# Fp16 halves of an attention kernel: a buffer and a DMA transpose per tile instead of per pair of tiles

## The chip, the cores and the metric

The kernel runs on 1 core of one Trainium2 chip. The metric is the time of one execution on the device in microseconds (us), the median of several runs; lower is better. A core has TensorE (PE, its weight loads PEld), VectorE (DVE), ScalarE (ACT), GpSimd (POOL) and SyncE (SP), which here only issues DMAs. Each engine works off its own instructions in order, and semaphores tie them together.

## The reference

Bucketed attention, then a mixing layer with a two-dimensional Fourier transform and a feed-forward network, then a gated layer:

```python
# q, k, v: (2, 8, 768, 64); proj: (64, 6); d_model = 512
q_bucket = np.sum((q @ proj > 0) * powers, axis=-1)      # the same for k
mask = q_bucket[:, :, :, None] == k_bucket[:, :, None, :]
scores = np.where(mask, scale * q @ k.T, -1e9)
attn = softmax(scores)
x = (attn @ v), heads side by side                       # (2, 768, 512)

mixed = np.real(fft(fft(x, axis=1), axis=2))
u = x + mixed
un = layer_norm(u)
x = u + np.maximum(un @ w_ch1, 0.0) @ w_ch2              # 512 -> 2048 -> 512

gate = sigmoid(causal depthwise convolution of x, 5 taps)
out = (gate * (x @ w_val)) @ w_out
```

## The kernel before

Matrix products are made in fp16 with each operand split into two halves, a high one (the value rounded to fp16) and a low one (the rest). Attention runs once for each of the two batches, `attention(b, ...)`. Of a batch's 8 heads two are taken together: a group `g` of 4. In a group the 768 query rows are three units `i` of two tiles of 128 rows; for each unit and each head `hh` of the group `pair` (L316) makes the softmax weights of two tiles `j`, and `unit_out` (L356) multiplies both heads' weights by the values `vt`.

One tile in `pair`: 4 matmuls into `sc` (L324), DVE moves the scores to `e` and takes the row maximum (L336), ACT makes the exponentials in `e` (L341) and then the high half in `a` (L345, by `copy_of`, L112), and POOL subtracts it from `e` to give the low half, in two instructions of 384 columns (L348, by `both`, L120). When both tiles of the pair are there, one DMA transpose issued by SP brings the whole of `a` (128 rows, 24 blocks of 128 columns) into `at` (L353). At 4 of the 48 places (`TPE`) the transpose is made by TensorE instead, in `by_pe` (L222): 24 transposes into three PSUM tiles of 1024 columns, and three copies by ACT. `unit_out` then runs 36 matmuls into `pv` (L362), which need all of `at` of both heads.

`prep(g)` (L230) does the like for a group's queries and keys: ACT writes the high halves of q and k into `st`, DVE (in part POOL) the low halves (L126, L120), one DMA transpose brings both into `tb` (L247), DVE copies parts of it to `ta` (L116), and matmuls into `bt` (L259) give the bucket codes. One group (`PPE`) goes by `by_pe`; the first group has its own `prep_first` (L279).

The pool `a` holds the buffers of `a` and `st`: 3 that last through both batches and 1 more during the first batch (L890, L894). `e` has 4 buffers in the first batch and 2 in the second; `at` 4 and 2.

SP issues every DMA of this part: the loads of q, k, v, the blocks of the large weights (`ring`, L431), which DVE, ACT and POOL turn into fp16 halves (L417 to L419 and the helpers), and the transposes. A `ring` load waits until its slot has been read. While the second batch's attention runs, TensorE works on the first batch's feed-forward matmuls (L710, L727). The program is built with a scheduler that orders each engine's instructions by an estimate of its own; `issue_after` fixes a few orders by hand.

## Time and profile before

| what | value |
|---|---|
| median of 3 runs | 696.27 us (696.04 to 697.73) |
| span of the profiled execution | 692.9 us |
| PE busy | 571.7 us, 83% |
| DVE busy | 518.3 us, 75% |
| ACT busy | 368.2 us, 53% |
| POOL busy | 290.5 us, 42% |
| DMA transposes `at<-a` | 44, median 5.9 us from issue to landing |
| DMA transposes `tb<-st` | 6, median 6.0 us |

The span runs from the first to the last instruction in one profiled execution; the time of a run is 3.4 us longer than that span. Busy shares are averages over stages of different kinds: to about 172 us the first batch's attention, then its mixing layer beside weights and the start of the second batch, to about 412 us the second batch's attention beside feed-forward matmuls, and then matrix products nearly alone.

### The profile page before, as it was taken

To read this page: it belongs to the slowest core of one execution; us is meant where nothing else is said; L and a number is where in the kernel's file an instruction comes from. 1 tells how busy PE (TensorE), PEld (TensorE's weight loads), DVE (VectorE), ACT (ScalarE), POOL (GpSimd) and SP (SyncE) were. 2 spreads that over 40 slices of the span, in tenths; PEclk is the share of its full clock that TensorE was granted. 3 is DMA by queue.
4 is the path that set the end of the run, shared out by engine and by line. 5 is a ranking of instruction groups with operands and counts; after the bars stand their busy time and mean duration, and the time that the engine had idled before them with its cause. 6 is when DMAs were issued, how large, how long until landed. Compare 5 with 4: busy or idle time off the path is not lost.

```text
span 692.9 us, 13096 instructions
## 1 busy us (share of the span) xinstructions
PE 571.7 (83%) x5078; PEld 439.0 (63%) x5078; DVE 518.3 (75%) x1007; ACT 368.2 (53%) x747; POOL 290.5 (42%) x312
## 2 busy tenths in 40 slices
PE   6667748677634868988789999899899999999997
PEld 2343516465423646766568789789676788888864
DVE  6888678778999888999965529987899346282582
ACT  4997779986765435876588815321244202111242
POOL 2857568875668523876556510244232100000000
PEclk9696859877866889999999999999999999999999
DMA  8879799895787452779667774100000000000001
GB/s 297 207 138 238 154 228 216 168 198 127 130 171 153 115 149 89 145 147 195 126 128 138 138 166 152 65 1 2 2 31 30 32 1 1 1 2 1 1 31 61
DMA packets 176284, 75.79 MB, mean 109 GB/s; under 512 B 160864, under 2 KB 166624, under 8 KB 176224
## 3 DMA queue, kind: packets, MB, share of 16 engines
q1 hardware_dynamic: 175648, 74.88, 48.6%
q8 instruction: 39, 0.64, 0.4%
q14 instruction: 21, 0.17, 0.1%
q10 hardware_dynamic: 576, 0.10, 0.1%
HBM read 32.50 MB, written 3.15 MB: 51 GB/s over the span
## 4 chain that ended last, share of the span: by engine, by line
PE 33%; DVE 30%; DMA 14%; issue 10%; POOL 7%; ACT 5%; SPq 0%; ACTq 0%; POOLq 0%; DVEq 0%
PE f L727 13%; DMA at<-a 8%; PE f L710 8%; POOL a L120 6%; DVE e L336 3%; DVE wt L417 3%; DVE wt L418 3%; PE pv L362 3%; DMA ring<-in_moe_w_ch_dram 3%; DVE gt L752 3%; DMA tb<-st 2%; PE op L871 2%; DVE wt L419 2%; ACT e L341 2%; PE vp L846 1%
## 5 line engine op out<-in xcount | busy, mean ns | idle before, releaser
L120 POOL TENSOR_TENSOR a<-e,a 128x384 f16<-128x384 f32 x184 | 177.0, 985 | 94.2 <-ACT a L112 60.9
L710 PE MATMUL f<-un,w 128*128 128x256 f16 x1152 | 137.5, 276 | 2.8 <-DVE h L692 2.4
L727 PE MATMUL f<-h,w 128*128 128x256 f16 x1152 | 131.6, 273 | 2.5 <-ACT w L112 2.5
L710 PEld LDWEIGHTS <-w 128*128 128x128 f16 x1152 | 113.7, 99 | 23.1 <-issue 5.1
L727 PEld LDWEIGHTS <-w 128*128 128x128 f16 x1152 | 111.8, 98 | 19.6 <-ACT w L112 2.8
L336 DVE TENSOR_SCALAR_CACHE_REDUCE e<-sc 128x768 f32<-128x768 f32 x96 | 91.0, 951 | 21.9 <-POOL a L120 17.4
L362 PE MATMUL pv<-at,vt 128*64 128x256 f16 x864 | 69.1, 304 | 39.8 <-DMA at<-a 32.3
L341 ACT ACTIVATE e<-e,mx 128x768 f32<-128x768 f32 x96 | 89.3, 931 | 3.8
L362 PEld LDWEIGHTS <-vt 128*64 128x64 f16 x864 | 56.2, 122 | 47.3 <-issue 31.3
L112 ACT ACTIVATE a<-e 128x768 f16<-128x768 f32 x96 | 80.3, 839 | 1.6 <-DMA at<-a 0.9
L324 PE MATMUL sc<-ta 96*128 96x384 f16 x192 | 54.8, 369 | 27.8 <-DVE e L336 24.7
L692 DVE SCALAR_TENSOR_TENSOR h<-f,h 128x512 f16<-128x512 f32 x48 | 32.7, 687 | 32.1 <-ACT h L691 32.0
L324 PE MATMUL sc<-tb 128*128 128x384 f16 x192 | 54.9, 370 | 0.0
L691 ACT ACTIVATE h<-f 128x512 f16<-128x512 f32 x48 | 28.3, 589 | 46.1 <-PE f L710 46.0
L120 POOL TENSOR_TENSOR w<-wt,w 128x256 f16<-128x256 f32 x40 | 31.3, 788 | 39.3 <-ACT w L112 39.3
L324 PEld LDWEIGHTS <-ta 96*128 96x128 f16 x192 | 17.4, 103 | 47.0 <-issue 40.6
L112 ACT ACTIVATE x<-xb 128x256 f16<-128x256 f32 x24 | 11.7, 536 | 62.5 <-DVE xb L698 61.1
L698 DVE SCALAR_TENSOR_TENSOR xb<-f,xb 128x256 f32<-128x256 f32 x24 | 13.7, 619 | 38.7 <-PE f L727 38.6
L340 ACT ACTIVATE mx<-mx 128x1 f32<-128x1 f32 x96 | 18.5, 197 | 39.4 <-DVE e L336 38.8
L417 DVE TENSOR_SCALAR wt<-ring 128x256 int32<-128x256 int32 (+1 forms) x60 | 32.5, 546 | 8.6 <-DMA ring<-in_moe_w_ch_dram 8.5
L418 DVE SCALAR_TENSOR_TENSOR wt<-ring,wt 128x256 int32<-128x256 int32 (+1 forms) x60 | 38.0, 638 | 0.6
L819 DVE SCALAR_TENSOR_TENSOR gt<-xb,cw,gt 128x256 f32<-128x256 f32 x60 | 37.3, 683 | 0.0
(147 smaller groups left out, 918.6 us busy)
## 6 DMA issues: line engine op xcount, KB each, us to landing
ring<-in_moe_w_ch_dram SPq DMA_DIRECT2D x40, 256.0 KB, 3.1
ring<-in_moe_w_ch_dram SPq DMA_DIRECT2D x12, 512.0 KB, 5.5
lv<-in_v_dram SPq DMA_DIRECT2D x8, 384.0 KB, 3.9
out_dram<-ob SPq DMA_DIRECT2D x12, 256.0 KB, 2.0
lq<-in_q_dram SPq DMA_DIRECT2D x7, 384.0 KB, 3.8
lk<-in_k_dram SPq DMA_DIRECT2D x7, 384.0 KB, 4.0
ring<-in_moe_w_val_dram SPq DMA_DIRECT2D x4, 512.0 KB, 4.1
ring<-in_moe_w_out_dram SPq DMA_DIRECT2D x4, 512.0 KB, 3.6
```

What stands on the lines that cost most here:

```text
L112: return nc.scalar.activation(out=o, in_=i, func=ACTF.Copy, scale=s)
L120: return (nc.gpsimd if eng == "g" else nc.vector).tensor_tensor(out=o, in0=i0, in1=i1, op=op)
L324: nc.tensor.matmul(out=s[:, n, 0:384], lhsT=z[0:rows, 0, hh, r], rhs=z[0:rows, 1, hh, n * 384:n * 384 + 384], start=(x == 0), stop=(x == 1),)
L336: nc.vector.tensor_scalar(e.rearrange("p (a b) -> p a b", a=2), s, -(PEN * PEN) / 2, None, ALU.max, ALU.max, accum_out=m[:, 0:1]).ins
L341: marks["first", 2 + j] = nc.scalar.activation(out=e, in_=e, func=ACTF.Exp, bias=m[:, 1:2], scale=SC, accum_out=sums[:, hh, j:j + 1]).ins
L362: nc.tensor.matmul(out=p[64 * hh:64 * hh + 64, :], lhsT=va[g][:, hh, c, x, :], rhs=at[hh][:, :, y, c, :], start=(c == 0 and n == 0), stop= ...
L417: nc.vector.tensor_scalar(tmp, hi, 3, 0x3FFFFFF8, ALU.logical_shift_left, ALU.bitwise_and)
L418: nc.vector.scalar_tensor_tensor(out=tmp, in0=hi, scalar=-0x40000000, in1=tmp, op0=ALU.bitwise_and, op1=ALU.bitwise_or)
L692: nc.vector.scalar_tensor_tensor(out=h[:, 1, f:f + 2, :], in0=p, scalar=0.0, in1=h[:, 0, f:f + 2, :], op0=ALU.max, op1=ALU.subtract)
L710: nc.tensor.matmul(out=p[:, o, :], lhsT=w1[:, i, kd, (f + o) * 128:(f + o) * 128 + 128], rhs=un[:, j, kd, :], start=(k == 0), stop=(k == 3 ...
L727: nc.tensor.matmul(out=p[:, o, :], lhsT=w2[:, i, f, (d + o) * 128:(d + o) * 128 + 128], rhs=h[:, j, f, :], start=(k == 0), stop=(k == 3 * ...
L819: nc.vector.scalar_tensor_tensor(out=o, in0=src, scalar=cw[:, d, j:j + 1].bitcast(FP32), in1=o, op0=ALU.mult, op1=ALU.add)
```

## The change

`a` becomes a buffer of one tile (both halves, 12 blocks of 128 columns), with 6 lasting buffers and 2 more in the first batch, so that the memory is the same. Each tile has a DMA transpose of its own into its half of `at`, issued for tile 0 without waiting for tile 1. `st` becomes two such buffers, one for q and one for k, each with its own transpose into its half of `tb`. `by_pe` handles one tile: two PSUM tiles of 768 columns and two copies, so four copies for a pair instead of three. The number of DMA transposes goes from 50 to 100; their bytes stay.

```diff
-TPE = {(0, g, i, 1): 'aaa' for g in range(4) for i in (1,)}
-PPE = {(0, 1): 'aaa'}
+TPE = {(0, g, i, 1): 'a' for g in range(4) for i in (1,)}
+PPE = {(0, 1): 'a'}
...
-        def by_pe(ot, it, how):
-            for o in range(0, 4 * S, 1024):
-                p = P.bt.tile([128, 1024], FP16, tag="g", name="atp") if b else P.tp.tile([128, 1024], FP16, tag="tp", name="atp")
-                for c in range(0, 1024, 128):
+        def by_pe(ot, it, eng):
+            for o in range(0, 2 * S, S):
+                p = P.tp.tile([128, 1024], FP16, tag="tp", name="atp")
+                for c in range(0, S, 128):
                     nc.tensor.transpose(p[:, c:c + 128], it[:, o + c:o + c + 128], P.idh)
-                i = copy_of(ot[:, o:o + 1024], p, 1.0, how[o // 1024])
+                i = copy_of(ot[:, o:o + S], p[:, 0:S], 1.0, eng)
             return i.ins
...
-                st = P.a.tile([128, 2, 2 * C, 2, D], FP16, tag="a", name="st", lasting=b and g == 0)
-                copy_of(st[:, 0, :, 1, :], lq, QS, "a")
-                copy_of(st[:, 1, :, 0, :], lk, QS, "a")
-                rest_of(st[:, 0, :, 0, :], st[:, 0, :, 1, :], lq, QS, REST[b][0])
-                rest_of(st[:, 1, :, 1, :], st[:, 1, :, 0, :], lk, QS, REST[b][1])
+                st = [P.a.tile([128, 2 * C, 2, D], FP16, tag="a", name="st", lasting=b and g == 0) for _ in range(2)]
+                for y, x in enumerate((lq, lk)):
+                    copy_of(st[y][:, :, 1 - y, :], x, QS, "a")
+                for y, x in enumerate((lq, lk)):
+                    rest_of(st[y][:, :, y, :], st[y][:, :, 1 - y, :], x, QS, REST[b][y])
...
-            if (b, g) in PPE:
-                it, ot = st.rearrange("p a c x d -> p (a c x d)"), tb.rearrange("p a h t -> p (a h t)")
-                marks[b, "prep", g] = by_pe(ot, it, PPE[b, g])
-            else:
-                marks[b, "prep", g] = nc.sync.dma_start_transpose(
-                    out=tb.rearrange("p a h (c t) -> p (a h c) t", t=128), in_=st.rearrange("p a c x d -> p (a c x d)")
-                ).ins
+            for y in range(2):
+                it = st[y].rearrange("p c x d -> p (c x d)")
+                if (b, g) in PPE:
+                    marks[b, "prep", g] = by_pe(tb[:, y].rearrange("p h t -> p (h t)"), it, PPE[b, g])
+                else:
+                    marks[b, "prep", g] = nc.sync.dma_start_transpose(
+                        out=tb[:, y].rearrange("p h (c t) -> p (h c) t", t=128), in_=it
+                    ).ins
...
-            a = P.a.tile([128, 2, 2, S], FP16, tag="a", name="a")
+            at = P.at.tile([128, 2, 2, C, 128], FP16, tag="at", name="at")
             for j in range(2):
+                a = P.a.tile([128, 2, S], FP16, tag="a", name="a")
...
-                copy_of(a[:, j, 0, :], e, 1.0, how[0])
+                copy_of(a[:, 0, :], e, 1.0, how[0])
...
-                    both(a[:, j, 1, w], e[:, w], a[:, j, 0, w], ALU.subtract, how[1])
-            at = P.at.tile([128, 2, 2, C, 128], FP16, tag="at", name="at")
-            if (b, g, i, hh) in TPE:
-                by_pe(at.rearrange("p j x c t -> p (j x c t)"), a.rearrange("p j x t -> p (j x t)"), TPE[b, g, i, hh])
-            else:
-                nc.sync.dma_start_transpose(out=at.rearrange("p j x c t -> p (j x c) t"), in_=a.rearrange("p j x t -> p (j x t)"))
+                    both(a[:, 1, w], e[:, w], a[:, 0, w], ALU.subtract, how[1])
+                it = a.rearrange("p x t -> p (x t)")
+                if (b, g, i, hh) in TPE:
+                    by_pe(at[:, j].rearrange("p x c t -> p (x c t)"), it, TPE[b, g, i, hh])
+                else:
+                    nc.sync.dma_start_transpose(out=at[:, j].rearrange("p x c t -> p (x c) t"), in_=it)
             return at
...
-        pools = AttnPools(base, ld=2, ta=2, tb=1, vt=2, e=2, a=3, at=2, sm=4, sc=2, pv=1, bt=1)
+        pools = AttnPools(base, ld=2, ta=2, tb=1, vt=2, e=2, a=6, at=2, sm=4, sc=2, pv=1, bt=1)
...
-        pools.widen(att, ld=1, tb=1, e=2, a=1, at=2)
+        pools.widen(att, ld=1, tb=1, e=2, a=2, at=2)
```

The scheduler orders the instructions anew. SP's queue in the first batch's attention, before (the numbers tell buffers apart; 128x24x128 is a whole pair, and `ring`, `lq` and `lk` are loads):

```order
L353 DMA_TRANSPOSE at_636<-a_611 128x24x128
L431 DMA ring_385<-in_moe_w_ch1_dram 128x1024 x2
L247 DMA_TRANSPOSE tb_724<-st_719 128x24x128
L353 DMA_TRANSPOSE at_663<-a_638 128x24x128
L213 DMA lk_765<-in_k_dram 128x2x384
L353 DMA_TRANSPOSE at_795<-a_770 128x24x128
```

and the same place of SP's queue after the change, where two buffers with one destination are the tiles of one pair:

```order
L355 DMA_TRANSPOSE at_623<-a_624 128x12x128
L355 DMA_TRANSPOSE at_623<-a_638 128x12x128
L355 DMA_TRANSPOSE at_652<-a_653 128x12x128
L433 DMA ring_390<-in_moe_w_ch1_dram 128x1024
L355 DMA_TRANSPOSE at_652<-a_667 128x12x128
L433 DMA ring_390<-in_moe_w_ch1_dram 128x1024
L248 DMA_TRANSPOSE tb_741<-st_735 128x12x128
L248 DMA_TRANSPOSE tb_741<-st_736 128x12x128
L211 DMA lq_782<-in_q_dram 128x12x64
```

The pair that stood behind the transpose of `st` now stands ahead of it, and a weight load stands between its two tiles. Later, in the second batch's attention while the weights `w2` are read, SP's queue before:

```order
L353 DMA_TRANSPOSE at_3185<-a_3160 128x24x128
L431 DMA ring2_2067<-in_moe_w_ch2_dram 128x512 x4
L353 DMA_TRANSPOSE at_3259<-a_3234 128x24x128
L353 DMA_TRANSPOSE at_3286<-a_3261 128x24x128
L431 DMA ring2_2067<-in_moe_w_ch2_dram 128x512 x2
L353 DMA_TRANSPOSE at_3359<-a_3335 128x24x128
```

and after the change:

```order
L433 DMA ring2_2128<-in_moe_w_ch2_dram 128x512 x3
L355 DMA_TRANSPOSE at_3315<-a_3316 128x12x128
L433 DMA ring2_2128<-in_moe_w_ch2_dram 128x512 x2
L355 DMA_TRANSPOSE at_3315<-a_3330 128x12x128
L355 DMA_TRANSPOSE at_3344<-a_3345 128x12x128
L355 DMA_TRANSPOSE at_3344<-a_3359 128x12x128
L433 DMA ring2_2128<-in_moe_w_ch2_dram 128x512 x2
L355 DMA_TRANSPOSE at_3420<-a_3421 128x12x128
L433 DMA ring2_2128<-in_moe_w_ch2_dram 128x512
L355 DMA_TRANSPOSE at_3420<-a_3434 128x12x128
```

Here loads that stood between pairs stand between the tiles of a pair. In the whole queue that is so at 8 of the 50 places, one in the first batch and seven in this stretch, with 11 loads between them.

## Rows read from the trace of the kernel before

**Rows 1.** The page, part 4: the ending chain's shares of the span by line
```profile
PE f L727 13%; DMA at<-a 8%; PE f L710 8%; POOL a L120 6%; DVE e L336 3%; DVE wt L417 3%; DVE wt L418 3%; PE pv L362 3%; DMA ring<-in_moe_w_ch_dram 3%; DVE gt L752 3%; DMA tb<-st 2%; PE op L871 2%; DVE wt L419 2%; ACT e L341 2%; PE vp L846 1%
```
**Rows 2.** Busy time by stage: PE, PEld, DVE, ACT, POOL, then PEclk, DMA share, GB/s
```profile
57.00:172.00 115.00, 82.56 (x754) 55.57 (x754) 89.32 (x165) 89.89 (x189) 81.52 (x83) 0.76 0.92 186
172.00:340.00 168.00, 119.08 (x1040) 87.69 (x1038) 154.46 (x304) 102.99 (x224) 100.52 (x106) 0.87 0.64 141
340.00:412.00 72.00, 65.20 (x640) 52.04 (x642) 36.27 (x72) 49.58 (x107) 35.87 (x41) 0.98 0.77 139
412.00:693.00 281.00, 267.07 (x2363) 223.45 (x2357) 192.19 (x378) 81.67 (x142) 37.65 (x32) 0.99 0.08 29
```
**Rows 3.** The ending chain from 50 to 175 us: start, length, what
```profile
57.62 5.48 DMA at<-a
...
67.15 7.44 DMA at<-a
...
90.82 10.07 DMA tb<-st
...
106.30 7.11 DMA at<-a
...
125.10 5.68 DMA at<-a
...
135.12 6.58 DMA at<-a
...
161.47 7.12 DMA at<-a
```
**Rows 4.** Transposes and their replacements by tile: ns min/median/max; landing counted from issue
```profile
L353 SPq DMA_TRANSPOSE at<-a x44: 3530/3900/5608, 23.8 to 403.8; - x44
L112 ACT ACTIVATE at<-atp x12: 997/1012/1056, 41.1 to 151.4; 128x1024 f16<-128x1024 f16 x12
...
DMA to landing us min/median/max: 5.4/5.9/8.2
```
```profile
L247 SPq DMA_TRANSPOSE tb<-st x6: 3689/4367/6664, 51.4 to 319.2; - x6
...
L112 ACT ACTIVATE tb<-stp x2: 792/792/792, 6.9 to 8.5; 128x768 f16<-128x768 f16 x2
```
**Rows 5.** SP's instructions in order of time: start, length
```profile
57.62 3.60 SPq L353 DMA_TRANSPOSE at<-a  x1
61.27 0.57 SPq L213 DMA_DIRECT2D lk<-in_k_dram  x1
62.01 4.34 SPq L353 DMA_TRANSPOSE at<-a  x1
66.46 0.52 SPq L431 DMA_DIRECT2D ring<-in_moe_w_ch_dram  x1
...
85.41 3.64 SPq L353 DMA_TRANSPOSE at<-a  x1
...
161.47 3.69 SPq L353 DMA_TRANSPOSE at<-a  x1
```
**Rows 6.** DMA issues from 57 to 172 us: count, median us to landing
```profile
at<-a SPq DMA_TRANSPOSE x16, 6.2
tb<-st SPq DMA_TRANSPOSE x3, 8.1
```
**Rows 7.** DVE from 54 to 104 us: the low halves of q and k
```profile
88.22 0.95 DVE L126 SCALAR_TENSOR_TENSOR st<-lq,st 128x768 f16<-128x768 f32 x1
89.08 1.67 DVE L126 SCALAR_TENSOR_TENSOR st<-lk,st 128x768 f16<-128x768 f32 x1
```
**Rows 8.** SP's waits from 172 to 340 us: total, times, longest
```profile
SPq L431 <- DVE wt L419: 43.5, 19, 5.6
```
**Rows 9.** Waits from 338 to 412 us: total, times, longest
```profile
DVE e L336 <- POOL a L120: 13.2, 11, 2.3
...
PE pv L362 <- DMA at<-a: 4.8, 4, 1.8
```

More of the change, by code (lines that the diff above doesn't have):

```diff
@@ L288, in prep_first @@
                 x = x[:, hh * C:hh * C + C]
-                st = P.a.tile([128, 2, 2 * C, 2, D], FP16, tag="a", name="st")[:, 0, 0:C]
+                st = P.a.tile([128, 2 * C, 2, D], FP16, tag="a", name="st")[:, 0:C]
                 copy_of(st[:, :, 1 - y, :], x, QS, "a")
```

## The prediction

> **What bounds the kernel now.** The chain that ended last comes first, for it says where the transposes that change lie on the path. Over the span, `DMA at<-a` has 8% of it and `DMA tb<-st` 2% [rows 1], about 69 us of 692.9 in all; that is the most that any change of the transposes could touch. The table by stage then shows what stands beside them. From 412 us on PE is busy for 267.1 of 281 us [rows 2]; no transposes run there, and this stage stays. From 340 to 412 us PE is busy for 65.2 of 72 us with feed-forward matmuls beside the second attention [rows 2]. From 172 to 340 us DVE is busy for 154.5 of 168 us [rows 2]: weights, mixing and attention share it, and only an idle share of 8% is left. The stage from 57 to 172 us is the odd one: PE, DVE, ACT and POOL are busy for 82.6, 89.3, 89.9 and 81.5 of 115 us, none above 78%, while the DMA share is 0.92 [rows 2]. In that stage the chain runs through six legs of `at<-a`, 5.48 to 7.44 us and 39.4 us together, and one leg of `tb<-st` of 10.07 us [rows 3]. So here the engines wait in turn for transposes, and what the change is worth is decided here.
>
> SP's own rows say why a leg is as long as it is. One transpose keeps SP for at least 3.53 us, 3.9 at the median, and its data has landed 5.4 us after the issue at least, 5.9 at the median [rows 4]: about 1.9 us behind the end of the issue. SP takes the next instruction 0.05 to 0.2 us after the last [rows 5], so the tail of 1.9 us lies beside the next issue, but the 3.9 us don't. From 57.6 to 67 us the queue is never empty: 3.60, 0.57, 4.34 and 0.52 us stand end to end [rows 5]. In the stage there are 16 transposes of `at` and 3 of `tb` [rows 6] and 17 loads: 16 times 3.9, 3 times 4.4 and 17 times 0.5 us are 84 of 115 us. SP is the busiest thing in the chain's neighbourhood, though not full.
>
> **The change part by part.** *What a transpose of one tile costs.* No row shows one of 12 blocks. The lower bound is half of the shortest, 1.8 us; the upper one is the whole, 3.6 us, if the time didn't depend on the size. The nearest row for a part that doesn't shrink is an ordinary load, which keeps SP for some 0.4 to 0.57 us [rows 5]. If 0.4 of the 3.6 us is such a part, a tile's issue is 0.4 + 1.6 = 2.0 us, which I take, with 0.1 us to the next instruction. A pair then keeps SP for 4.2 us instead of 3.7: 0.5 us more. For 19 pairs in the stage from 57 to 172 us that is 9.5 us of SP's time, and SP has 31 us free there.
>
> The trace's row for the rest of a DMA is the 1.9 us between end of issue and landing, and it lies beside the next issue. The Trainium skill, "DMA: Bandwidth & Descriptors", section "Rules for kernel authors", advises the opposite of this change: many small transfers should be coalesced into one, and its section on the anatomy of a DMA puts the fixed part at about 2.0 us. Were such a part paid in series, the 19 added transposes of this stage would cost 38 us, an estimate by that page's figure. The rows, in which the next issue doesn't wait for a landing, speak against paying it so, and no run here shows a half yet.
>
> *What a leg loses.* The last tile of a pair has 2.0 + 1.9 = 3.9 us to land instead of 5.9, provided tile 0's transpose left earlier, which it does where SP is free. So a leg that begins with SP idle becomes 2.0 us shorter, less some 0.4 us that the extra issue cost puts ahead of it: 1.6 us. Three legs are like that, 125.10, 135.12 and 161.47 [rows 3]: 4.8 us. The legs at 57.62, 67.15 and 106.30 stand in runs of issues without a gap, where the whole run only starts about 2 us earlier and then loses 0.5 us for each pair; I give 1.0 us for the three together. For `tb`, q's low half is done at 89.1 us and k's at 90.8 [rows 7], so q's transpose can leave 1.7 us earlier; less the extra cost that is 1.0 us. Sum: 6.8 us. Not all of it arrives: DVE has 25.7 us idle in the stage [rows 2], so it doesn't forbid it, but the DMA share of 0.92 leaves only 9.2 us of the 115 to be saved with the same bytes, and in the runs another engine is close behind. I take 4.5 us.
>
> *Does it last?* Behind 172 us DVE does the same number of instructions; what it gets earlier it finishes earlier, so the 4.5 us go through to the matmul stage. There the legs sit under a different limit: of 340 to 412 us DVE waits 13.2 us for POOL to free an `e` buffer [rows 9], and `e` keeps 2 buffers, so the pairs' pace doesn't change. PE's waits for `at`, 4.8 us in 4 pieces [rows 9], get shorter by up to 1.6 us each; since PE has other work and the `e` loop sets when the next pair comes, I take 0.5 us.
>
> *The small edits.* `by_pe` needs 20 copies by ACT where it needed 15: 20 times 0.79 (the row of 768 columns) is 15.8 us against 15 times 1.01 or 15.2 us [rows 4], 0.6 us over five places, hidden by ACT's 25 idle us in the main stage [rows 2]; without that cover it would cost the 0.6 us. The buffers of `a` hold as many tiles as before and are freed a tile at a time; a wait for one is no piece among the legs of the stage that matters [rows 3], so I give it nothing. The wait for a free `at` buffer now stands ahead of tile 0, with tile 1's transpose and the next load behind it on SP and PE's `pv` waiting for them; before, it stood ahead of the pair, so the same buffer is waited for no longer than it was: nothing again.
>
> *The new order.* The scheduler has moved everything a little. PE's counts at the ends of units are almost those of before; by the last unit of the second attention PE has done 680 feed-forward matmuls instead of 654, which moves PE work forward and adds none. I price it at zero, with some 5 us either way for the range, a guess as large as the term that is forecast.
>
> Sum: 692.9 - 4.5 - 0.5 = 687.9 us for the span, and with the 3.4 us that a median run takes beyond it 691.3 us.
>
> **The rivals.** *The legs give way to the next thing in line.* In 57 to 172 us ACT and DVE are at 78%, and the run of issues stays as long because the bytes stay. Then what is saved at one leg is waited for at the next: 694.2 to 698.4 us. For it speaks the DMA share of 0.92; against it that all four engines are idle together at the legs.
>
> *Loads between the tiles hold SP.* At 8 places a `ring` load now stands between the two tiles of a pair, 11 loads in all. SP works in order, so a load whose slot isn't free keeps the second tile's transpose, and with it PE's `pv`, waiting. From 172 to 340 us such waits came 19 times with 43.5 us, 2.3 us each [rows 8]. If each of the 11 loads waits that long, second tiles are held for 25 us; with half of that on the path and the 5 us of gain kept, the time is 696.3 - 5 + 12.6 = 704 us. It decides from the point at which the 11 loads cost more than 5 us together, under 0.5 us each. Against it: second tiles come later than first ones anyway, so a load may be waited for while nothing is ready. This is the case that ends slower.
>
> *A tile's transpose doesn't cost half.* At 2.6 us with 0.1 us behind it, 38 of them and 8.5 us of loads make 111 us of SP's 115, and the gain is gone; at 3.6 us they make 149 us, so that the stage grows by 34 us and the time is 730 us. What speaks against it is that an issue of 3.5 us can hardly be anything but the blocks, since a load with 128 rows needs 0.4 us [rows 5]. The rule of the Trainium skill's DMA page quoted above points to this case.
>
> *All legs shorten in full.* 7 legs in the main stage by 1.9 us are 13.3 us, but the DMA share caps them at 9.2; with PE's 4.8 us [rows 9] gone too, and the new order giving some, 682 us and a little below.
>
> **How the numbers follow.** Forecast, 686 to 694.1 us: 0.40. All legs in full, 678 to 686: 0.15. Given to the next in line, within 0.3% (2.1 us, about what a measurement of this kernel can tell from no change), 694.2 to 698.4: 0.17. Loads between the tiles, 698.5 to 706: 0.21. A tile costs much more than half, above 704: 0.07. So faster 0.55, same 0.17, slower 0.28. The range of 8 in 10 leaves out the lower part of the full gain, the upper part of the loads' case and the last rival: 681 to 702 us. The likeliest sign's own range is 681 to 694.1 us.
>
> **What would show it.** Rows of the changed kernel: `at<-a` 88 times at about 2.0 us of issue, 3.9 us to landing, `tb<-st` 12 times. `DMA at<-a` should have fallen from 8% of the chain to about 6%, with the legs of 57 to 172 us at 4 to 5 us. DVE's idle time up to 172 us should be some 4 us less, and the 340 to 412 us stage end about 5 us earlier at the same length. If issues are 2.5 us or more, the third rival holds; if SP shows long waits of `ring` loads with a transpose behind them and PE waits there for `at`, the second. If legs are shorter but DVE's and ACT's waits for other things grow by as much, the first. The forecast is wrong too where the new order alone moves the stages behind 172 us by more than 5 us.

## The result and the profile after

| | kernel before | changed kernel |
|---|---|---|
| median of 4 runs each | 696.15 us (693.99 to 697.73) | 683.42 us (682.47 to 685.87) |
| ratio | | 0.9831, 95% interval 0.9806 to 0.9855 |
| span of the profiled execution | 692.9 us | 681.0 us |

The changed kernel is faster by 12.7 us. The forecast was 691.3 us, 5 us faster: the sign was right and the time lies in the range, but the gain is two and a half times the one that was worked out. The question behind it is which of its steps was too small.

Three events of PE's timeline cut the span: the first `zp` matmul, with which the mixing layer begins; the first feed-forward matmul `f`; and the end. At `zp` eleven of the twelve units of the first attention are through (396 of its 432 `pv` matmuls; 391 in e11_nine_buffers and 365 in n5_e11, of the experiments below); the last unit still comes behind it. The rows of the timeline that hold the first two (start, length), before:

```profile
157.88 0.22 PE L501 MATMUL zp<-cf,y 128*128 128x128 f16 x1
...
252.02 4.23 PE L710 MATMUL f<-un,w 128*128 128x256 f16 x19
```

and after:

```profile
146.73 0.22 PE L503 MATMUL zp<-cf,y 128*128 128x128 f16 x1
...
242.60 0.61 PE L712 MATMUL f<-un,w 128*128 128x256 f16 x4
```

So 11.2 us are gained up to `zp`, 1.8 us are given back up to `f` (9.4 gained), and 2.5 us more come between `f` and the end. The last unit's `pv` matmuls, which end the first attention, before:

```profile
168.63 2.13 PE L362 MATMUL pv<-at,vt 128*64 128x256 f16 x35 [0.24 <-DMA at<-a]
```

and after:

```profile
157.76 2.13 PE L364 MATMUL pv<-at,vt 128*64 128x256 f16 x17
```

They end 10.9 us earlier. The busy time of the same stages as in [rows 2] (the last ends with the shorter span):

```profile
57.00:172.00 115.00, 84.84 (x775) 55.74 (x773) 100.77 (x185) 96.10 (x203) 84.56 (x87) 0.83 1.02 198
172.00:340.00 168.00, 126.87 (x1100) 93.54 (x1095) 154.52 (x301) 105.70 (x233) 99.96 (x113) 0.86 0.67 144
340.00:412.00 72.00, 70.81 (x714) 58.45 (x712) 40.16 (x80) 44.03 (x89) 26.43 (x30) 1.00 0.67 136
412.00:681.00 269.00, 253.28 (x2183) 210.17 (x2181) 182.67 (x351) 74.05 (x135) 36.56 (x32) 0.98 0.06 22
```

Between 57 and 172 us DVE is busy for 100.8 us where it was 89.3 [rows 2], ACT for 96.1 instead of 89.9. The stage that was named as the place of the gain is where the engines now wait less, though the same stretch now also holds 25 us behind `zp` where it held 14. The DMA share reads 1.02, so the 0.92 of before was no cap of 9.2 us. The transposes themselves, by tile (SP's issue: ns min/median/max; then ACT's copies of `by_pe`; then the time from issue to landing), answer [rows 4]:

```profile
L355 SPq DMA_TRANSPOSE at<-a x88: 1273/1722/4027, 20.8 to 391.6; - x88
L112 ACT ACTIVATE at<-atp x16: 787/798/842, 35.0 to 139.4; 128x768 f16<-128x768 f16 x16
...
DMA to landing us min/median/max: 3.7/4.2/6.9
```

```profile
L248 SPq DMA_TRANSPOSE tb<-st x12: 1414/1776/2922, 51.3 to 319.8; - x12
```

And rows of POOL and SP (start, length), the counterpart of [rows 5]:

```profile
117.69 7.17 POOL L120 TENSOR_TENSOR a<-e,a 128x384 f16<-128x384 f32 x8 [0.38 <-DVE xb L380]
...
119.50 6.99 SPq L355 DMA_TRANSPOSE at<-a  x4
...
142.87 1.41 SPq L355 DMA_TRANSPOSE at<-a  x1
...
147.90 1.43 SPq L355 DMA_TRANSPOSE at<-a  x1
```

A lone transpose takes 1.4 us. Four in a row take 6.99 us, but there POOL sets the pace: its eight subtractions, two to a tile, take 7.17 us. By the medians a pair keeps SP for 3.4 us, where one transpose of the pair took 3.9 us. What PE waits for in the first attention (total, times, longest) shows where that arrives; the kernel before, up to 157.9 us:

```profile
PE pv L362 <- DMA at<-a: 17.0, 9, 4.0
PE sc L324 <- DVE e L336: 14.7, 14, 3.4
PE bt L259 <- DMA tb<-st: 6.0, 2, 3.0
```

and the changed one, up to 146.7 us:

```profile
PE sc L326 <- DVE e L338: 16.5, 16, 2.4
PE pv L364 <- DMA at<-a: 7.2, 5, 3.0
PE bt L260 <- DMA tb<-st: 2.2, 2, 2.0
```

PE's waits for transposed data fall from 23.0 to 9.4 us. In two other orders of both kernels, described below, the same sum goes from 23.4 to 12.9 us (n10) and from 16.4 to 16.0 us (n5), so its fall depends on the order. In this profile the ending chain is followed back only to about 340 us and holds no transpose, so it can't be laid beside [rows 1] and [rows 3].

### The profile page after: what moved, and what is told of

It reads as the page before. It is cut to its first block, busy times and chain, and to the rows that moved or that the text cites. A ratio compares the mean times of both kernels' runs of the same rounds, so it can differ in the third digit from the quotient of the medians.

```text
span 681.0 us, 13258 instructions
## 1 busy us (share of the span) xinstructions
PE 578.8 (85%) x5078; PEld 443.7 (65%) x5078; DVE 521.9 (77%) x1007; ACT 367.0 (54%) x752; POOL 283.4 (42%) x312
## 4 chain that ended last, share of the span: by engine, by line
PE 30%; DVE 13%; ACT 3%; issue 3%; POOL 1%; ACTq 0%; DVEq 0%; POOLq 0%
PE f L729 14%; PE f L712 8%; DVE gt L754 3%; PE op L873 2%; PE vp L848 1%; PE vp L770 1%; ACT a L112 1%; PE op L795 1%; DVE x L126 1%; DVE gt L117 1%; DVE h L694 1%; ACT e L343 1%; DVE cen L644 1%; PE mp L601 1%; DVE gt L821 1%
## 5 line engine op out<-in xcount | busy, mean ns | idle before, releaser
L120 POOL TENSOR_TENSOR a<-e,a 128x384 f16<-128x384 f32 x184 | 174.9, 976 | 93.0 <-ACT a L112 75.7
L712 PE MATMUL f<-un,w 128*128 128x256 f16 x1152 | 135.3, 274 | 3.2 <-DVE h L694 2.7
L729 PE MATMUL f<-h,w 128*128 128x256 f16 x1152 | 133.1, 274 | 0.9 <-DVE h L694 0.9
L338 DVE TENSOR_SCALAR_CACHE_REDUCE e<-sc 128x768 f32<-128x768 f32 x96 | 90.5, 949 | 16.1 <-POOL a L120 12.6
L364 PE MATMUL pv<-at,vt 128*64 128x256 f16 x864 | 75.3, 323 | 26.4 <-DMA at<-a 23.4
L364 PEld LDWEIGHTS <-vt 128*64 128x64 f16 x864 | 58.0, 130 | 44.7 <-issue 23.7
L326 PE MATMUL sc<-ta 96*128 96x384 f16 x192 | 51.4, 352 | 29.8 <-DVE e L338 26.0
L326 PE MATMUL sc<-tb 128*128 128x384 f16 x192 | 51.9, 353 | 0.0
L420 DVE SCALAR_TENSOR_TENSOR wt<-ring,wt 128x256 int32<-128x256 int32 (+1 forms) x60 | 37.0, 623 | 0.6
L112 ACT ACTIVATE wt<-wt 128x256 f32<-128x256 f32 x40 | 16.2, 412 | 37.7 <-DVE wt L421 36.7
L421 DVE SCALAR_TENSOR_TENSOR wt<-ring,wt 128x256 int32<-128x256 int32 (+1 forms) x60 | 35.7, 602 | 0.5
```

What stands on the lines that cost most here:

```text
L112: return nc.scalar.activation(out=o, in_=i, func=ACTF.Copy, scale=s)
L120: return (nc.gpsimd if eng == "g" else nc.vector).tensor_tensor(out=o, in0=i0, in1=i1, op=op)
L326: nc.tensor.matmul(out=s[:, n, 0:384], lhsT=z[0:rows, 0, hh, r], rhs=z[0:rows, 1, hh, n * 384:n * 384 + 384], start=(x == 0), stop=(x == 1),)
L338: nc.vector.tensor_scalar(e.rearrange("p (a b) -> p a b", a=2), s, -(PEN * PEN) / 2, None, ALU.max, ALU.max, accum_out=m[:, 0:1]).ins
L364: nc.tensor.matmul(out=p[64 * hh:64 * hh + 64, :], lhsT=va[g][:, hh, c, x, :], rhs=at[hh][:, :, y, c, :], start=(c == 0 and n == 0), stop= ...
L420: nc.vector.scalar_tensor_tensor(out=tmp, in0=hi, scalar=-0x40000000, in1=tmp, op0=ALU.bitwise_and, op1=ALU.bitwise_or)
```

## The experiments

Two parts of the change could make the legs shorter: that a transpose is short (S), or that tile 0's transpose starts before tile 1 is there (E). Beside them stand the buffers of one tile, `by_pe` with four copies, and the new order of all engines. The table gives all runs; medians, ratios against the kernel before on the same chip (which took 696.0 to 697.2 us on the chips of the experiments), and the last three columns from each profiled execution.

| kernel | median us | ratio (95%) | first `zp` | first `f` | `f` to the end |
|---|---|---|---|---|---|
| before | 696.15 | | 157.9 | 252.0 | 440.9 |
| after | 683.42 | 0.9831 (0.9806 to 0.9855) | 146.7 | 242.6 | 438.4 |
| e1_two_dmas | 696.29 | 1.0004 (0.9984 to 1.0023) | 152.5 | 251.1 | 442.8 |
| e2_cols | 687.37 | 0.9865 (0.9825 to 0.9905) | 152.1 | 250.7 | 432.9 |
| e3_at_only | 693.96 | 0.9954 (0.9925 to 0.9984) | 150.4 | 248.0 | 441.8 |
| e4_st_only | 696.38 | 1.0011 (0.9987 to 1.0036) | 160.2 | 254.3 | 439.8 |
| e8_pair_buffers | 691.76 | 0.9942 (0.9913 to 0.9972) | 148.4 | 247.2 | 441.3 |
| e11_nine_buffers | 697.21 | 1.0019 (0.9994 to 1.0043) | 148.6 | 245.4 | 450.8 |
| e12_seven | 698.25 | 1.0041 (1.0012 to 1.0070) | 160.4 | 249.6 | 449.6 |
| e6_few_buffers | 702.86 | 1.0096 (1.0066 to 1.0127) | 162.9 | 253.6 | 445.3 |
| e5_halves | 709.00 | 1.0187 (1.0150 to 1.0225) | 153.7 | 249.9 | 454.8 |
| e7_by_pe | 707.96 | 1.0167 (1.0132 to 1.0201) | 167.6 | 263.4 | 445.7 |
| n5_before | 692.09 | 0.9952 (0.9922 to 0.9982) | 155.0 | 246.5 | 441.1 |
| n10_before | 702.07 | 1.0075 (1.0049 to 1.0101) | 155.8 | 258.6 | 438.5 |
| n2_after | 683.50 | 0.9829 (0.9806 to 0.9852) | 147.4 | 244.2 | 438.9 |
| n5_after | 694.22 | 0.9974 (0.9950 to 0.9999) | 150.2 | 244.3 | 446.4 |
| n10_after | 689.29 | 0.9888 (0.9856 to 0.9920) | 152.5 | 244.8 | 443.4 |
| n5_e8 | 692.35 | 0.9945 (0.9922 to 0.9967) | 151.8 | 247.2 | 443.4 |
| n5_e11 | 685.57 | 0.9834 (0.9789 to 0.9878) | 152.8 | 248.2 | 436.6 |
| n5_e1 | 689.88 | 0.9906 (0.9877 to 0.9935) | 147.7 | 247.8 | 442.9 |

**Two transposes for a pair.** e1_two_dmas is the kernel before with two transposes, written behind the loop over the tiles, and two for `st`:

```diff
-                nc.sync.dma_start_transpose(out=at.rearrange("p j x c t -> p (j x c) t"), in_=a.rearrange("p j x t -> p (j x t)"))
+                for j in range(2):
+                    nc.sync.dma_start_transpose(out=at[:, j].rearrange("p x c t -> p (x c) t"), in_=a[:, j].rearrange("p x t -> p (x t)"))
```

> The kernel before with its pair buffers kept, but two DMA transposes per pair, one per tile, and two for q and k. Theory E (the first tile's transpose leaves before the second tile is made, which shortens the legs): all of the gain, about 684 us. Theory S (two short transposes hold SP for less time than one long one, 1.4 to 1.8 us each against 3.6 to 3.9): about 684 us too. Rival B (the gain comes from buffers that are freed a tile at a time): stays near 696 us.

e2_cols lays the pair out by column halves, so that each of its two transposes needs both tiles; `st` stays whole:

```diff
-            a = P.a.tile([128, 2, 2, S], FP16, tag="a", name="a")
+            a = P.a.tile([128, 2, 2, 2, S // 2], FP16, tag="a", name="a")
...
-                nc.sync.dma_start_transpose(out=at.rearrange("p j x c t -> p (j x c) t"), in_=a.rearrange("p j x t -> p (j x t)"))
+                for w in range(2):
+                    nc.sync.dma_start_transpose(out=at[:, w].rearrange("p j x c t -> p (j x c) t"), in_=a[:, w].rearrange("p j x t -> p (j x t)"))
```

> The kernel before with pair buffers whose columns are laid out in two halves: two DMA transposes per pair, each with half the columns of both tiles, so that neither can leave before the second tile's exponentials are made and the first is ready only about 0.9 us before the second. q and k keep one transpose. Theory E: nearly nothing, 693 to 697 us. Theory S: most of the gain, 684 to 688 us, with issues of 1.4 to 1.8 us. Rival O (the order that the scheduler happens to find): anywhere from 680 to 705 us.

`zp` came 5.4 us earlier than before in e1 and 5.8 us earlier in e2. e1 turned out not to tell S from E: its transposes stand behind the loop, but each waits for its own tile only. The rows of SP and of POOL (start, length) show one leaving at 119.92 us, after two of the four subtractions that run in the 3.54 us from 118.09 and with them one tile:

```profile
119.92 3.20 SPq L355 DMA_TRANSPOSE at<-a  x2
```

```profile
118.09 3.54 POOL L120 TENSOR_TENSOR a<-e,a 128x384 f16<-128x384 f32 x4 [4.48 <-DMA at<-a]
```

e2 doesn't tell them apart either. Its first transpose needs only the first 384 columns of tile 1, and where SP is free it leaves before POOL has subtracted the other 384. Rows of one such place in each kernel follow: POOL's last subtraction of a pair, SP's transposes, and the time from the last issue to landing. The kernel before:

```profile
124.16 0.91 POOL L120 TENSOR_TENSOR a<-e,a 128x384 f16<-128x384 f32 x1
125.10 3.53 SPq L353 DMA_TRANSPOSE at<-a  x1
DMA to landing us min/median/max: 5.7/5.7/5.7
```

e2_cols:

```profile
119.38 0.91 POOL L120 TENSOR_TENSOR a<-e,a 128x384 f16<-128x384 f32 x1
119.45 1.43 SPq L354 DMA_TRANSPOSE at<-a  x1
120.97 1.75 SPq L354 DMA_TRANSPOSE at<-a  x1
DMA to landing us min/median/max: 4.3/4.3/4.3
```

The changed kernel, with both subtractions of tile 1:

```profile
119.48 1.79 POOL L120 TENSOR_TENSOR a<-e,a 128x384 f16<-128x384 f32 x2
119.50 1.43 SPq L355 DMA_TRANSPOSE at<-a  x1
121.30 1.48 SPq L355 DMA_TRANSPOSE at<-a  x1
DMA to landing us min/median/max: 3.8/3.8/3.8
```

From the end of the last subtraction to the last landing it is 5.7, 4.9 and 3.8 us; from the first issue to the last landing 5.7, 5.8 and 5.6 us. So in these places, with SP free, two short transposes are no faster than one long one, and the leg is shorter by as much as the first of them leaves early: some 0.85 us in e2 and 1.8 us in the changed kernel. That is E. e2 is early in a second way: `unit_out` takes the columns in order, so its first matmuls need only the first transposes, and here PE begins 2 us before the second has landed:

```profile
123.26 4.05 PE L363 MATMUL pv<-at,vt 128*64 128x256 f16 x35 [0.48 <-DMA at<-a]
```

What S adds where transposes queue up on SP, these two runs don't separate. The whole times were 696.3 and 687.4 us: e1 had lost its 5 us again by the first `f`, e2 had found more behind it. That was the first sign that something else moves the end by as much as the change.

**`at` alone and `st` alone.** e3_at_only is the kernel before with e1's edit to `at`, shown above, and `st` whole; e4_st_only is the kernel before with this alone:

```diff
-                marks[b, "prep", g] = nc.sync.dma_start_transpose(
-                    out=tb.rearrange("p a h (c t) -> p (a h c) t", t=128), in_=st.rearrange("p a c x d -> p (a c x d)")
-                ).ins
+                for y in range(2):
+                    marks[b, "prep", g] = nc.sync.dma_start_transpose(
+                        out=tb[:, y].rearrange("p h (c t) -> p (h c) t", t=128), in_=st[:, y].rearrange("p c x d -> p (c x d)")
+                    ).ins
```

> The kernel before with two DMA transposes per pair of attention tiles, one transpose still for q and k together. Both E and S: 685 to 688 us, since 44 of the 50 places are of this kind and six of the seven legs of 57 to 172 us. Rival O: it need not lie between before and after at all.

> The kernel before with two DMA transposes for q and k, one still per pair of attention tiles. E and S: 693 to 695 us, the one leg of 10 us in the first attention shortened by 2 us and little more. Rival O: 690 to 702 us without a pattern.

With `at` alone `zp` comes at 150.4 us, with `st` alone at 160.2, later than before. The gain up to `zp` belongs to `at`; the 1.0 us forecast for `tb` is not to be seen.

**The buffers.** e8_pair_buffers is the change in all but its buffers, which hold a pair again:

```diff
+            ap = P.a.tile([128, 2, 2, S], FP16, tag="a", name="a")
             for j in range(2):
-                a = P.a.tile([128, 2, S], FP16, tag="a", name="a")
+                a = ap[:, j]
```

The others are the change with another number of tile buffers, in place of 6 lasting ones and 2 more: 4 and 1 in e6_few_buffers, 6 and 1 in e12_seven, 6 and 3 in e11_nine_buffers; of e11:

```diff
-        pools.widen(att, ld=1, tb=1, e=2, a=2, at=2)
+        pools.widen(att, ld=1, tb=1, e=2, a=3, at=2)
```

> The changed kernel in all but the buffers: a pair's two tiles share one buffer again (3 lasting and 1 more), and q and k share one. Transposes are issued tile by tile, inside the loop. Theory B (the half of the gain that two transposes alone don't bring comes from buffers freed by tile): 692 to 696 us, with the first attention's end (first matmul of the mixing layer) near 152 us instead of 146.7. Rival P (what matters is where the transposes and the destination stand in the program, since the scheduler follows it): 683 to 686 us. Rival O (each build's order is a draw): no relation to either, 683 to 700.

> The changed kernel with 4 lasting tile buffers and 1 more in the first batch instead of 6 and 2. Theory B: slower than the changed kernel, 688 to 697 us, above all in the first attention. Rival O: within a few us of 683 either way, with the first attention as fast.

> The changed kernel with 1 more tile buffer in the first batch instead of 2, seven in all. Theory B: between eight (683.4) and five (702.9), 685 to 692 us, the first attention 1 to 6 us longer. Rival O: no order by the number of buffers.

> The changed kernel with 3 more tile buffers in the first batch instead of 2, nine in all. Theory B: buffers still bind a little, 680 to 683 us; if eight are enough for the lifetimes: 682 to 686 us. Five of them cost 20 us.

e8 took 691.8 us, which looked as if the buffers were worth 8.4 us. But nine buffers, one more than the change has, took 697.2, with nearly the same `zp` (148.6 us) and a feed-forward stage of 450.8 us in place of 438.4. With five and seven, `zp` came at 162.9 and 160.4 us, later than in any kernel with short transposes and more room; yet part of that is work that the scheduler moved. Busy time up to `zp` (PE, PEld, DVE, ACT, POOL), of the changed kernel and of e6_few_buffers:

```profile
0.00:146.70 146.70, 110.64 (x956) 69.99 (x957) 119.44 (x232) 125.42 (x264) 103.53 (x125) 0.81 1.02 217
```

```profile
0.00:162.90 162.90, 115.59 (x956) 71.33 (x957) 137.66 (x251) 131.57 (x279) 115.92 (x136) 0.79 0.95 214
```

DVE does 18.2 us more before `zp` there, and `zp` to `f` is 5.2 us shorter for it (90.7 against 95.9 us). What fewer buffers cost by themselves stays open.

**Parts with other work.** e5_halves is the change cut on: a tile's high half and low half each get a transpose, 176 of 6 blocks, the first issued when the high half is there. e7_by_pe is the kernel before with only `by_pe`'s copies as after, 768 columns and four for a pair:

```diff
                 copy_of(a[:, 0, :], e, 1.0, how[0])
+                if (b, g, i, hh) not in TPE:
+                    nc.sync.dma_start_transpose(out=at[:, j, 0], in_=a[:, 0, :])
...
-                    nc.sync.dma_start_transpose(out=at[:, j].rearrange("p x c t -> p (x c) t"), in_=it)
+                    nc.sync.dma_start_transpose(out=at[:, j, 1], in_=a[:, 1, :])
```

```diff
-            for o in range(0, 4 * S, 1024):
+            for o in range(0, 4 * S, S):
...
-                i = copy_of(ot[:, o:o + 1024], p, 1.0, how[o // 1024])
+                i = copy_of(ot[:, o:o + S], p[:, 0:S], 1.0, how[0])
```

> The changed kernel with the high and the low half of each attention tile transposed apart: 176 transposes of 6 blocks for at instead of 88 of 12. Theory S (SP's time goes by the blocks, with little that is fixed): issues of 0.7 to 0.9 us and a time of 679 to 685 us, the last leg shorter by another 0.5 to 0.9 us. If each DMA has a fixed part of 0.4 us or more on SP: the first attention gets 3 to 6 us longer and the time is 686 to 692 us.

> The kernel before with only the new by_pe: PSUM tiles of 768 columns and four copies for a pair instead of three of 1024. By its own cost nothing: 696 to 697 us. Rival O: a move of 3 us or more either way shows how much a build's order alone is worth.

SP's issues in e5_halves, by tile (high halves, low halves):

```profile
L349 SPq DMA_TRANSPOSE at<-a x88: 1209/1238/2480, 17.9 to 422.1; - x88
L357 SPq DMA_TRANSPOSE at<-a x88: 1209/1274/2439, 20.0 to 423.5; - x88
```

Six blocks cost SP 1.24 to 1.27 us and twelve 1.72 at the median (least 1.21 and 1.27), so the second cut saves less than half a microsecond per transpose and doubles their number: by the medians 176 of them are about 221 us of SP where 88 are 152 (44 of 24 blocks were 172). The kernel was 1.87% slower than before. e7 was slower by 1.67%, though its copies are 0.6 us more in all. In its first attention DVE waits longer for the scores than it did before; DVE's waits up to `zp`, of e7_by_pe and of the kernel before:

```profile
DVE e L336 <- PE sc L324: 12.0, 5, 7.4
```

```profile
DVE e L336 <- PE sc L324: 4.0, 6, 1.7
```

One wait of 7.4 us, with DVE idle for PE's scores, would make up most of the 9.7 us by which its `zp` is late; that it stood on the path isn't shown. Whether the copies or the order put it there these two runs can't tell.

**The order by itself.** Three edits change which instruction is written first and nothing that is computed or moved: q's low half directly behind q's copy (n2), k's copy and low half ahead of q's (n5), k loaded ahead of q from the second group on (n10). The scheduler answers n5 and n10 with another order of every engine; n2 changes little.

n5 in the changed kernel, and n10 in both:

```diff
-                for y, x in enumerate((lq, lk)):
+                for y, x in ((1, lk), (0, lq)):
                     copy_of(st[y][:, :, 1 - y, :], x, QS, "a")
-                for y, x in enumerate((lq, lk)):
                     rest_of(st[y][:, :, y, :], st[y][:, :, 1 - y, :], x, QS, REST[b][y])
```

```diff
-            parts = [(0, slice(0, 1)), (1, slice(0, 1)), (0, slice(1, 2)), (1, slice(1, 2))] if not (b or g) else [(0, slice(0, 2)), (1, slice(0, 2))]
+            parts = [(0, slice(0, 1)), (1, slice(0, 1)), (0, slice(1, 2)), (1, slice(1, 2))] if not (b or g) else [(1, slice(0, 2)), (0, slice(0, 2))]
```

> The kernel before with k's copy and low half written ahead of q's in prep: the same instructions and waits, another order on every engine. It measures what a build's order alone is worth. Rival O: 4 us or more away from 696. If the order is worth little: 694 to 698 us.

> The changed kernel with q's low half written directly behind q's copy in prep, ahead of k's copy: the same work, another order on every engine. Rival O: 4 us or more away from 683.4. If the gain is the short transposes' and buffers' own: 681 to 687 us, and the first attention ends (first matmul of the mixing layer) within 3 us of 146.7.

> The changed kernel with k's copy and low half written ahead of q's: the same work, another order of every engine. If the change's gain is its transposes and its buffers, a second order stays near the first: 680 to 688 us, with the first mixing matmul at 145 to 149 us. If several us of the gain are the order that the first build happened to get, this one lies at 688 to 698 us, with the stage of feed-forward matmuls 5 us and more longer than the 438.4 us of the first.

> The change in all but its buffers (they hold a pair), with k's copy and low half written ahead of q's. If the buffers are worth the 8.4 us that lie between 691.8 and 683.4, this draw stays at 689 to 695 us and above the second draw of the change. If that was the order, the two families lie among each other: a time under 687 us, or the change's second draw above this one.

> The change with three more buffers in the first block in place of two, with k's copy and low half written ahead of q's. If the ninth buffer itself cost the 13.8 us between 683.4 and 697.2, this draw stays above 693 us. If it was the order behind the first attention (the first mixing matmul came at 148.6 us there, with the feed-forward stage at 450.8 us), this draw comes to 683 to 691 us with that stage at 436 to 444 us.

> Pair buffers, two transposes for a pair issued after both tiles, with k's copy and low half written ahead of q's. If the 12.9 us between it and the change (696.3 against 683.4) are buffers and early first transposes, it stays at 692 to 700 us. If the first draw lost its 5.4 us of the first attention again by a bad order, it comes to 687 to 691 us, with the first mixing matmul again at 150 to 153 us.

> The kernel before with k loaded ahead of q from the second group on: the same work, a third order. If its time is set by the order as much as that of the changed kernel, it lies anywhere from 690 to 699 us; the first mixing matmul comes at 154 to 161 us, since the transposes of pairs stay. A time under 688 us would mean that pairs lose nothing.

> The changed kernel with k loaded ahead of q from the second group on: a third order. If the transposes of tiles are worth 5 to 8 us in the first attention whatever the order, its first mixing matmul comes at 146 to 153 us, 4 to 10 us ahead of the kernel before with the same edit; the whole time may be anything from 683 to 695 us, with the feed-forward stage from 436 to 450 us. If tiles give nothing of their own, both first mixing matmuls come within 3 us of each other.

This settled most of it. The changed kernel takes 683.4, 694.2 and 689.3 us in three orders, and the kernel before 696.2, 692.1 and 702.1. Order by order the change gains 12.7 us in the first and 12.8 in n10; in n5 it is 2.1 us slower, with ratios whose intervals overlap (0.9950 to 0.9999 and 0.9922 to 0.9982). Nine buffers go from 697.2 to 685.6 by the same edit that takes eight from 683.4 to 694.2. Pair buffers stay at 692 (e8), and go from 696.3 to 689.9 (e1). An edit that does nothing moves a kernel by 0.1 to 11.6 us.

What holds whatever the order is the first attention, up to `zp`. `zp` comes at 157.9, 155.0 and 155.8 us before and at 146.7, 150.2 and 152.5 after: 156.2 against 149.8 in the mean, 6.4 us with a standard error of 1.9. Leave out the kernels with other work or less room (e5, e6, e7, e12) and n2_after, which is nearly the order of after. Then the eleven whose `at` comes by transposes of 12 blocks have `zp` between 146.7 and 152.8 us, the four with 24 blocks (e4_st_only among them) between 155.0 and 160.2. The legs themselves say the same. From a pair's last subtraction to the landing of its last transpose, in the mean of the 20 pairs of the first batch that go by DMA, it is 8.1 to 8.8 us in the four and 6.0 to 7.2 us in the eleven (8.7 before, 6.4 after, 7.2 in e2). Buffers of a tile (five kernels, mean 150.2) and of a pair (six, 150.5) don't differ at `zp`. At `f` the five are 3.6 us ahead (245.1 and 248.7, standard error 1.2), a comparison picked afterwards, and by the end it is lost.

Some of the 6.4 us is work put off: DVE is busy for 124.1 us up to `zp` in the mean of the three orders before and for 121.9 after. The last `pv` of the first attention ends at 170.8, 167.7 and 177.3 us before and at 159.9, 157.5 and 160.9 after, 12.5 us earlier in the mean, but with 5.9 us less of DVE's work ahead of it; so `zp` is the fairer mark.

What doesn't hold is the rest. From `f` to the end every kernel runs the same 3654 matmuls. Busy time in that stage (PE, PEld, DVE, ACT, POOL, the granted clock), for six of them. The kernel before:

```profile
252.00:692.90 440.90, 408.04 (x3654) 332.19 (x3650) 307.80 (x601) 187.13 (x377) 124.27 (x130) 0.98 0.30 68
```

after:

```profile
242.60:681.00 438.40, 410.73 (x3654) 332.43 (x3650) 310.50 (x599) 185.41 (x375) 122.73 (x128) 0.98 0.30 68
```

n5_before:

```profile
246.50:687.60 441.10, 409.88 (x3654) 332.67 (x3650) 305.38 (x604) 187.67 (x378) 128.95 (x130) 0.98 0.30 69
```

n5_after:

```profile
244.30:690.70 446.40, 413.47 (x3654) 334.56 (x3650) 311.65 (x597) 186.06 (x374) 123.21 (x128) 0.97 0.30 66
```

e11_nine_buffers:

```profile
245.40:696.20 450.80, 419.15 (x3654) 338.26 (x3650) 315.98 (x603) 188.25 (x379) 125.12 (x131) 0.96 0.29 67
```

n5_e11:

```profile
248.20:684.80 436.60, 406.81 (x3654) 331.79 (x3650) 306.23 (x596) 185.85 (x374) 124.44 (x128) 0.98 0.30 68
```

The stage takes 436.6 to 450.8 us in these six. Between the two orders of nine buffers 12.3 of the 14.2 us are PE's own busy time, 419.2 against 406.8 us for the same matmuls, at a granted clock of 0.96 against 0.98; the rest is PE idle, 31.7 against 29.8 us. Between after and n5_after 2.7 of the 8.0 us are busy time and 5.3 are idle (27.7 and 32.9 us). One stretch of e11 in which the clock fell to the lower of its two levels (1.2 of 2.4 GHz), and the one ahead of it, in which PE was busy for 3.44 of 6.8 us:

```profile
332.50:339.30 6.80, 3.44 (x35) 2.01 (x37) 6.35 (x11) 4.97 (x10) 3.58 (x4) 1.00 0.90 160
339.30:349.50 10.20, 9.04 (x64) 5.40 (x58) 7.27 (x15) 7.76 (x17) 6.07 (x8) 0.50 0.30 56
```

So an order costs in two ways: by matmuls that run while the clock is granted low, and by waits.

## Why the prediction was off, point by point

**Where the gain is.** Right. The stage of the first attention, SP's transposes and PE's waits for `at` were named; the eleven and the four kernels above differ in that stage, in every order, and in no other as clearly. The chain of n5_after, which is followed back to 43.5 us, is the nearest to [rows 1]:

```profile
PE f L729 14%; PE f L712 12%; POOL a L120 5%; PE pv L364 4%; DMA at<-a 4%; DVE wt L420 3%; DVE wt L421 3%; DVE e L338 3%; PE sc L326 2%; DMA ring<-in_moe_w_ch_dram 2%; PE op L873 2%; DVE gt L754 2%; DVE wt L419 2%; DMA tb<-st 2%; DVE cen L644 1%
```

`DMA at<-a` has 4% where it had 8, and about 6 was forecast; `DMA tb<-st` keeps its 2%. But the chain of n10_before, whose transposes are of whole pairs, has 4% as well:

```profile
PE f L727 13%; PE f L710 9%; POOL a L120 5%; DVE e L336 4%; DMA at<-a 4%; DMA tb<-st 3%; ACT e L341 3%; DVE gt L752 3%; DVE wt L417 2%; DVE wt L418 2%; PE pv L362 2%; DVE wt L419 2%; PE op L871 2%; ACT a L112 2%; DVE ta L116 2%
```

So the share goes by the order too, and doesn't show the change.

**The price of a tile's transpose.** Too high, beyond its bounds. The text took 2.0 us between 1.8 and 3.6, on the ground that half of 3.53 can't be undercut. The median is 1.72 us, a lone one 1.4 and the least 1.27: the time falls by more than the blocks do between 24 and 12, and by less between 12 and 6 (1.72 to some 1.25 at the median, 1.27 to 1.21 at the least). The 0.5 us that each pair was to cost SP more, 9.5 us in the stage, isn't there: by the medians a pair costs 3.4 us instead of 3.9.

The Trainium skill, "DMA: Bandwidth & Descriptors", section "Rules for kernel authors", advises coalescing many small transfers, and names 64 KB as the size under which a transfer is mostly overhead. A tile of 12 blocks is 393 KB (128 rows of 1536 fp16 values), so the rule doesn't speak against this change; SP's time per pair fell. The cut to 6 blocks, 197 KB, was dear on SP well above that size: 2.5 us per tile in place of 1.7. The figure of 2.0 us behind the estimate of 38 us stands in the Trainium skill, "DMA: Bandwidth & Descriptors", in the section "Anatomy of one DMA", for DMAs that GpSimd issues; here SP issues them, and the 38 us weren't paid.

**The legs.** Mechanism right, size too small. That a leg with SP idle gets 1.6 us shorter because tile 0's transpose leaves early is what the three places above show: 3.8 us from the last subtraction to landing in place of 5.7. The sum of 6.8 us was cut to 4.5, mostly because a DMA share of 0.92 was read as leaving 9.2 us. The share went to 1.02, and the mean gain at `zp` is 6.4 us, though one of the three legs counted, the one at 161.47 us, lies behind `zp`. `tb` was given 1.0 us; e4_st_only gained nothing.

**Does it last.** It was to go through behind 172 us. In the mean of three orders it does up to `f` (252.4 against 243.9 us, 8.5 with a standard error of 3.6), and no more comes after: `f` to the end is 440.2 us before and 442.7 after (2.6 longer, standard error 2.5), so the 0.5 us forecast for the second attention can't be seen. DVE's wait for POOL to free `e`, given as the limit there, was shorter in the first order; 338 to 412 us of the changed kernel, against 13.2 us in [rows 9]:

```profile
DVE e L338 <- POOL a L120: 8.5, 9, 2.0
```

Over the whole program it is 17.4, 10.6 and 19.4 us in the three orders before and 12.6, 14.0 and 13.8 after, so this too goes by the order.

**The small edits.** `by_pe`: 787 to 842 ns a copy as taken, and 16 and 4 of them. "Hidden" stays unproved: e7, which has this edit alone, is slower than every order of before, though the changed kernel has it too and shows no such loss.

**The new order, priced at zero with 5 us either way: the step that failed.** In the first build this term was worth 5 to 7 us, as much as the legs. The mean time of the eleven kernels with short transposes is 691.0 us and that of the four with long ones 696.7, a difference of 5.6 us with a standard error of 2.4; over the three orders of each kernel it is 7.8 us with one of 4.3. Within these errors the change's own worth is about what was forecast. The rest of the 12.7 us, 4.9 to 7.1, is the order that the first build drew: its 683.4 us is the least of the eleven, whose standard deviation is 4.4 us, and two orders of one kernel differ by up to 11.6. The text had called its 5 us either way a guess as large as the term that was forecast, and nothing in the profile before gave it a sign, so zero was a fair centre; what was wrong was to expect some 5 us from one build, when the order of that build can add or take as much again. That the change measured two and a half times its forecast was luck, and so in part was that it lay in the range: the lower end, 681 us, had been given to legs that shorten in full and not to an order. A smaller slip: the 3.4 us between span and median compares a median with one profiled run, while the profiled runs of the experiments lie 1.7 to 2.5 us above their spans; the forecast, 5.0 us below the median before, doesn't depend on it.

**The rivals.** Legs that give way to the next thing in line: e1 did that in both its orders. Against the kernel before in the same order 5.4 us were gained at `zp` and 0.9 left at `f`, and in n5 7.3 were gained and 1.3 lost. The changed kernel kept 9.4, 2.2 and 13.8 us at `f`. Whether pair buffers are the reason wasn't tested. Loads between the tiles: the wait that was named was longer in the first order. SP's wait row from 172 to 340 us, against 43.5 us in [rows 8]:

```profile
SPq L433 <- DVE wt L421: 52.3, 22, 4.9
```

All waits of `ring` loads in that stretch together are 73.4 us before and 70.8 after in this order, 60.9 and 87.9 in n5, 79.0 and 85.1 in n10. PE's total wait for `at` fell over the program in all three, from 32.3 us to 23.4 in the first, so little of it reached PE. The rival in which a tile doesn't cost half was wrong by the rows above. All legs in full, 682 us, is nearest to the time, for another reason than its own: it needed 9.2 us from the first attention in every order, and got 11.2 in one and 6.4 in the mean.

**What stays open.** What an order does to the end wasn't foreseen from anything in the profile before, and isn't explained here beyond clock and waits. Whether tile buffers are worth anything (mean time of five kernels 689.9 us, of six with pair buffers 691.9) is below what these runs can tell. E is shown where SP is free; no run has short transposes with neither part early, so what S adds where transposes queue up stays open.

## What to carry to other kernels

When a scheduler orders the program anew after each edit, measure two or three neutral rewrites of both versions before believing a gain of a per cent: here one such edit was worth up to 11.6 us, more than the change. Judge the mechanism where it acts, by an event near the end of its stage (`zp` here), since that number kept its sign in every order when the whole time did not. And where a long transfer sits between two engines, try it in two: the leg ends sooner by as much as the first part can leave ahead of the last work, as long as the issue of the parts isn't dearer than that of the whole. An experiment that is to keep both parts from leaving early should be checked in its trace for whether it does.

## What the runs showed of the hardware

- The time for which a DMA transpose keeps SP is far from proportional: 3.53 us at least for 24 blocks of 128 columns (median 3.90), 1.27 for 12 (1.72) and 1.21 for 6 (1.24 to 1.27). Landing came 5.9, 4.2 and 3.1 us after the issue at the median.
- In the places shown, with SP free, two transposes of 12 blocks had landed 5.8 us (e2_cols) and 5.6 us (changed kernel) after the first issue, one of 24 after 5.7.
- The mean busy share of the 16 DMA engines can stand at 1.02 over 115 us, so 0.92 was no ceiling to compute with.
- The same 3654 matmuls took PE 406.8 to 419.2 us, with a granted clock of 0.98 to 0.96 in the mean of the stage (n5_e11 and e11_nine_buffers).
